# Infini-attention and a GELU FFN on one core: small operations moved off VectorE, first tiles projected in five parts, 64-row rests of twelve weight tiles in one bracket

## The chip, the cores and the metric

The kernel runs on one core of one Trainium2 chip. A core has TensorE (PE: matmuls and transposes, which write into eight PSUM banks of 128 x 2 KB), VectorE (DVE), ScalarE (ACT: activations from tables that must be loaded), GpSimd (POOL) and SyncE (SP), which issues most of the DMAs here. The metric is the time of one execution in microseconds (us). Every time below is the chip's, from timed runs or from one profiled execution.

## The reference

Input x is 2048 x 576 in bf16. LN is a layer norm without weights. There are 32 heads of 18, and the rows are cut into four segments of 512.

```python
def _A_ref(x, wq, wk, wv, wo, beta):
    q, k, v = (heads(x @ w) for w in (wq, wk, wv))       # heads() stands for reshape and transpose
    phi = lambda t: jnp.where(t > 0, t + 1.0, jnp.exp(t))
    g = _sigmoid(beta).reshape(1, H, 1, 1)
    for s in range(N):                                   # the four segments, M and z start at 0
        logits = einsum('bhqd,bhkd->bhqk', qs, ks) * scale + mask
        a_dot = einsum('bhqk,bhkd->bhqd', _softmax(logits), vs)
        a_mem = einsum('bhld,bhde->bhle', phi(qs), M) / (einsum('bhld,bhd->bhl', phi(qs), z)[..., None] + 1e-06)
        outs.append(g * a_mem + (1.0 - g) * a_dot)
        M = M + einsum('bhld,bhle->bhde', phi(ks), vs)
        z = z + einsum('bhld->bhd', phi(ks))
    return concat(outs) @ wo

h  = x + _A_ref(LN(x), wq, wk, wv, wo, beta)
h2 = h + (gelu(LN(h) @ w1 + b1) @ w2 + b2)               # w1 576 x 4608, w2 4608 x 576
```

## The kernel before

**Units.** The rows are cut into 8 chunks of 256, two tiles of 128 rows each; a segment is two chunks. A contraction over 576 is four blocks of 128 rows and a rest of 64. `mm5` (L720 to 723) is such a group: four matmuls of 128 rows (L722) and one for the rest (L723). F1 (the product with w1) is computed transposed: 36 column tiles of w1 times 256 rows of x make a chunk's hT; what the code calls a half is two of those tiles in one PSUM bank, ten matmuls of 128x256, and its eviction adds b1 (L1284 by ScalarE, L1286 by VectorE). F2 then contracts 36 blocks of hT with w2, 288 columns at a time (L1376).

**Streams.** The kernel is a planner. Python generators emit operations: P (LN, transposes, projections of a tile), K and M (phi(k) and the memory's sums), A (scores L957, exp L974, mask L978, weighted values L997), the recall from memory (L1026 to L1034) and what ends a block (L1043 to L1053), B (output projection, residual, second LN), F1 and F2. Each operation has a planned duration and a due time (the tables SLACK, PHASES and LATE). `step` takes the earliest due operation of a ready engine; `either` (L471) gives an eviction to VectorE or ScalarE, whichever is planned to be free first. At the end all operations are issued in the order of their planned start under a manual schedule, so every engine's order is fixed when the program is built, and the waits between engines follow from which tile each operation reads and writes.

**PSUM.** Scores of a visit fill st4, one tile of four banks. `ox` and `bank0` to `bank2` are tiles of one bank each; projections, transposes, F1, F2 and the output projection take turns on bank0 to bank2, and on ox once attention is finished.

**Row tiles.** Score matmuls use 32 rows of the array at a time, a 64-row rest can use 64 (`Half.tail`, L1214; two tiles of weights sit at rows 0 to 63 and 64 to 127). Ten times a pair of halves puts its rests (`pair.tails`) next to a score visit and its full matmuls (`Half.main`, L1220) behind. All other halves compute the rest as a fifth full matmul over rows that are zero in the weights.

**Head.** While nothing is ready in the first microseconds, TensorE multiplies zeros (L1424). x of the first tiles, wq, wk and wv arrive by SP's queue; LN is two bn_stats, bn_aggr (L733), two small operations on VectorE (L734, L735), a power on GpSimd (L740) and the normalisation on VectorE (L743) or ScalarE (L748). In either case one more small copy repeats 64 columns (L745). The normalised tile is transposed by TensorE for the first tiles (pe_x and its like in SLACK say how many) and by a DMA for the others. A tile's projection is four groups of 432 columns; their evictions are at L844 to L854, the transposes of Q and K at L874 and the copies out at L877. Zeros for the paddings are written by GpSimd and VectorE (`memset`, L625). The memory's mask (`maskcol`, `gmzm`) is applied at L926 and after.

**Weights.** w2 stays in SBUF. w1 comes again for each chunk, 512 columns at a time (L1192: 512 KB, L1195: twice 32 KB), two buffers deep, five in the first chunk.

Of the kernel before, what the change touches and what calls it, by code (L numbers as in the profile page):

```python
# [8 lines left out]
ACT = mybir.ActivationFunctionType  # L9
# [7 lines left out]
def kernel(  # L17
# [41 lines left out]
    def sbuf(name, shape, dt=BF16):  # L59
# [13 lines left out]
    SLACK = dict(head=2.35, lnp=15.71, lnb=4.06, pow=-3.98, apply=7.94, ek_k=78.96, relu_k=-8.71, min_k=3.71,  # L73
                 add_k=10.93, mz=14.56, exp=16.96, ek=21.6, relu=47.98, min=14.06, add=31.72, hb=57.84,
                 gelu=30.88, finish=-1.23, mem=0.08, sum=20.21, out=3.91, hd=34.06, xp=-29.81, xb=-19.31,
                 t_x=23.19, t_q=37.57, t_k=38.16, t_o=-3.03, t_h=19.9, w1=3.76, w2=33.77, hc=-2.46, evict=-17.31,
                 qk=7.8, ot=-7.54, mask=0.42, lead=1.57, balance=22.63, b1=11.77, zeros=6.77, hold=0.62,
                 delay=0.92, pe_x=2, pe_q=3, pe_k=2, pe_o=2, pe_h=1, d_x1=1.69, d_wk=-5.24, marg=0.8, cj=4,
                 flex=1.0, qkv=0.0, flexn=1.0, d_wv=1.68, d_xb=0.5, d_wo=3, d_b2=1.97, bulk=11.07, w2v=5)
    PHASES = [(30.0, dict(exp=38.12, hold=2.18, sum=8.51, lnp=15.18, min_k=9.68, lead=1.93, t_h=47.5, t_o=-3.5,  # L80
                          flexn=1.85, mem=25.71)),
              (60.0, dict(gelu=28.89, apply=7.66, min_k=-36.61, lnp=16.16, w2=14.91, qk=8.17, t_q=37.57, delay=0,
                          hc=9.3)),
              (110.0, dict(t_x=30.47, min=14.15, mz=13.94, hold=5.27, w1=24.51, t_q=28.42, ek=20.74, apply=0.43,
                          pow=-9.03, xp=-16.35, hc=0.85, w2=31.47, out=4.0, bulk=8.26)),
              (200.0, dict(mem=-1.42, w1=12.55, lead=3.33, t_o=-5.89, mask=8.5, finish=-0.41, xb=-20.35, hd=32.92,
                          lnb=4.83, exp=20.2, apply=21.55)),
              (300.0, dict(add_k=6.54, delay=0.17, add=4.0, hd=24.4, mem=3.13, mz=15.86, ek_k=80.69, min_k=14.3,
                          exp=16.63, join=-18.57, qk=4.56, lead=1.87, xp=-30.24, min=9.66, qkv=5.33, t_x=21.9,
                          out=37.08, apply=10.19, hold=0.28))]  # L90
# [81 lines left out]
    def note(o, rd, wr):  # L172
# [5 lines left out]
        for k in rd:  # L178
# [4 lines left out]
        'wqkv0': [0.2],  # L183
        'mhalf': [4.1],
        'wqkv_pad': [4.4],
# [14 lines left out]
        ('x_p', 0): [0, 15.2, 41.5, 77.3, 169.5, 193.4, 233.4],  # L200
        ('qk', 0, 'pad'): [17.5],
        'wqkv1': [1.4],
        ('v1', 0): [22.7],
        ('v1', 1): [26.9],
        'ident': [4.9],
        ('v1', 2): [45.5],
        ('v1', 3): [57.3],
        'wqkv1t': [1],
        ('v1', 4): [60.2],
        ('v1', 5): [67.5],  # L210
        'maskcol': [58.4, 70.6, 62.4, 71.3, 63.8],
        ('qk', 2, 'pad'): [24.9],
        ('x_p', 1): [2, 26.1, 91.6, 103.7, 202.6, 212.6, 294.4],
        ('v1', 6): [123.5],
        'beta': [29.3],
        'wqkv2': [3.5],
        'wqkv2t': [3.7],
        ('o', 0, 'pad'): [27.9],
        ('x_b', 0): [7.6, 30.5, 71.9, 119, 172.9, 230.9, 273.1, 317.9, 377.7],
        ('phik', 0, 'pad'): [32.7],  # L220
        ('wo', 4): [38.2, 44],
        ('phik', 1, 'pad'): [33.8],
        ('w1', 0, 'z', 0): [41.5],
        ('x_b', 1): [10.9, 45, 87.4, 133.1, 201.2, 242.8, 296.4, 330.6, 418],
        ('w1', 0, 'z', 1): [39.6],
        'stp0': [2.8, 3.3, 3.8, 4.3, 11, 11.5, 11.9, 12.5, 21.5, 23.3, 21.5, 22.3, 51.2, 47.3, 36.4, 25.7,
            78.9, 94.5, 95.4, 97.9, 174.1, 174.5, 175, 175.5, 195.3, 194.5, 193.8, 196.7, 244.8, 239.6,
            247.2, 236.5],
        ('w1', 1, 'z', 0): [44.9],
        'b1': [18.1],  # L230
        ('w1m', 2, 'z', 1): [46.3],
        ('wo', 0): [23.5],
        ('w1m', 2, 'z', 0): [59],
        ('w1', 1, 'z', 1): [53.3],
        ('qk', 3, 'pad'): [57.8],
        ('o', 1, 'pad'): [48.3],
        ('xn1', 0): [5, 13.2, 25.8, 49.4, 89.7, 176.2, 197.5, 238.4],
        ('w1m', 3, 'z', 1): [58.4],
        ('w1m', 3, 'z', 0): [58.7],
        ('w1m', 4, 'z', 1): [66],  # L240
        ('xT', 'p', 0): [5.2, 16.9, 22.9, 46.4, 90.3, 177.4, 198.5, 245.7],
        'MZb': [71.1, 69, 72.3, 71.4, 71.7, 76.8, 64.6, 74.2, 62.6, 191.3, 192.4, 192.2, 195.4, 196.6, 197.4,
# [1240 lines left out]
```

## Time and profile before

| | us |
|---|---|
| three timed runs: lowest, median, highest | 476.8, 477.23, 478.39 |
| the profiled execution | 476.5 |
| its span in the trace | 474.8 |
| exp of the scores (L974), 80 on ScalarE | 150.2 busy |
| F2 (L1376), 1044 and more on TensorE | 144.0 busy |
| evictions of F1 (L1286), 130 on VectorE | 89.3 busy, 0.688 each |
| gelu (L1349), 23 on ScalarE | 66.0 busy |

The page's second section cuts the span into 40 slices of 11.9 us and gives busy tenths; these are VectorE's, ScalarE's and GpSimd's:

```profile
DVE  4889996587877476888877556887457646334310
ACT  2578879964678668896789595687457864212210
POOL 9468463295745344786773518665133312000000
```

A digit of 9 is 90% or more. The largest lines of VectorE are the evictions of F1, of ScalarE the exponentials:

```profile
L974 ACT ACTIVATE pt<-st 128x2048 bf16<-128x2048 f32 x80 | 150.2, 1877 | 65.4 <-PE st L957 63.6
L1286 DVE TENSOR_TENSOR hT<-bank,b1T 128x512 bf16<-128x512 f32 x130 | 89.3, 688 | 72.5 <-PE bank L723 65.1
L1043 DVE STREAM_TRANSPOSE ox<-ox 128x512 f32<-128x512 f32 x32 | 23.2, 725 | 11.7 <-PE ox L997 11.1
```

Such a line reads: place in the code, engine, operation, output and input, count; then busy us in all and mean ns of one; then the engine's idle time before them and what ended most of it.

### The profile page before, as it was taken

How to read it: one execution, taken by the hardware profiler on the slowest of the kernel's cores; microseconds unless marked ns; L12 is line 12 of the kernel's file. 1: busy time of each engine (PE TensorE's matmuls, PEld its weight loads, DVE VectorE, ACT ScalarE, POOL GpSimd, SP SyncE). 2: the span in 40 equal slices, each digit the busy share in tenths (PEclk: the TensorE clock that was granted, in tenths of full speed). 3: DMA queues.
4: the chain of work that ended last, by engine and by line, in shares of the span. 5: the costliest groups of instructions: out<-in, count | busy, mean ns of one | idle time of the engine just before them, and what ended most of it. 6: DMA issues, size and time to landing. Idle time of an engine off the chain costs nothing.

```text
span 474.8 us, 14410 instructions
## 1 busy us (share of the span) xinstructions
PE 462.5 (97%) x6056; PEld 350.9 (74%) x6056; DVE 311.4 (66%) x744; ACT 302.9 (64%) x245; POOL 217.2 (46%) x333
## 2 busy tenths in 40 slices
PE   8999999799999999999999999999999999999997
PEld 6655687468777777767768777777877788888875
DVE  4889996587877476888877556887457646334310
ACT  2578879964678668896789595687457864212210
POOL 9468463295745344786773518665133312000000
PEclk9999999999999999999999999999999999999999
DMA  8999799927588577469458559486744655655411
GB/s 240 200 231 206 262 163 295 253 52 165 162 214 218 150 178 185 97 142 199 83 155 204 156 143 193 89 196 187 181 147 135 185 166 158 185 168 164 137 39 50
DMA packets 118881, 79.94 MB, mean 168 GB/s; under 512 B 53344, under 2 KB 116768, under 8 KB 118816
## 3 DMA queue, kind: packets, MB, share of 16 engines
q1 hardware_dynamic: 118784, 79.01, 66.8%
q8 instruction: 47, 0.77, 0.7%
q14 instruction: 18, 0.15, 0.1%
q0 software_dynamic: 32, 0.01, 0.1%
HBM read 60.09 MB, written 7.08 MB: 141 GB/s over the span
## 4 chain that ended last, share of the span: by engine, by line
PE 84%; DVE 6%; ACT 4%; issue 2%; DMA 2%; SPq 1%; ACTq 0%; DVEq 0%
PE bank L722 29%; PE bank L1376 26%; PE bank L723 7%; PE st L957 5%; PE ox L997 4%; PE bank L1220 4%; PE ox L1376 3%; PE st L1424 2%; DMA xT<-xn 2%; ACT pt L974 1%; PE ox L722 1%; PE bank L1026 1%; ACT hT L1349 1%; DVE ox L1043 1%; PE bank L1214 1%
## 5 line engine op out<-in xcount | busy, mean ns | idle before, releaser
L974 ACT ACTIVATE pt<-st 128x2048 bf16<-128x2048 f32 x80 | 150.2, 1877 | 65.4 <-PE st L957 63.6
L1376 PE MATMUL bank<-w_sb,hT 128*128 128x288 bf16 x1044 | 144.0, 286 | 2.1 <-ACT hT L1349 2.1
L1286 DVE TENSOR_TENSOR hT<-bank,b1T 128x512 bf16<-128x512 f32 x130 | 89.3, 688 | 72.5 <-PE bank L723 65.1
L1376 PEld LDWEIGHTS <-hT 128*128 128x128 bf16 x1152 | 110.5, 98 | 31.8 <-ACT hT L1349 2.4
L978 POOL TENSOR_SCALAR_AFFINE_SELECT pt<-pt 128x512 bf16<-128x512 bf16 x128 | 80.4, 643 | 107.1 <-ACT pt L974 105.4
L722 PE MATMUL bank<-xn2T,w1g 128*128 128x256 bf16 (+1 forms) x888 | 122.2, 269 | 1.9 <-DMA w1g<-in_B_w_dram 0.9
L722 PEld LDWEIGHTS <-w1g 128*128 128x128 bf16 x944 | 88.4, 98 | 16.3 <-issue 1.5
L1349 ACT ACTIVATE hT<-hT 128x4608 bf16<-128x4608 bf16 (+5 forms) x23 | 66.0, 2874 | 46.7 <-DVE hT L1286 46.5
L723 PE MATMUL bank<-xn2T,w1g 128*128 128x256 bf16 (+1 forms) x222 | 59.7, 269 | 0.0
L722 PE MATMUL bank<-wqkv,xT 128*128 128x432 bf16 x256 | 57.4, 346 | 1.1 <-DMA xT<-xn 0.8
L722 PEld LDWEIGHTS <-xT 128*128 128x128 bf16 x384 | 34.9, 97 | 23.7 <-DMA xT<-xn 0.9
L1016 POOL TENSOR_TENSOR pq<-ek,pq 128x512 bf16<-128x512 bf16 x24 | 27.9, 1163 | 11.8 <-DVE ek L1014 9.1
L957 PE MATMUL st<-QT,KT 32*128 32x128 bf16 x1280 | 32.2, 217 | 1.2 <-ACT pt L974 1.1
L1043 DVE STREAM_TRANSPOSE ox<-ox 128x512 f32<-128x512 f32 x32 | 23.2, 725 | 11.7 <-PE ox L997 11.1
L1380 DVE TENSOR_TENSOR ot<-bank,hc 128x288 bf16<-128x288 f32 x29 | 13.1, 453 | 25.1 <-PE bank L1376 25.1
L957 PEld LDWEIGHTS <-KT 32*128 32x128 bf16 x1280 | 18.8, 92 | 14.3 <-issue 9.2
L997 PE MATMUL ox<-pt,v_aug 128*19 128x128 bf16 x1280 | 26.5, 220 | 0.0
L997 PEld LDWEIGHTS <-v_aug 128*19 128x19 bf16 x1280 | 17.9, 91 | 10.9 <-issue 10.0
L723 PEld LDWEIGHTS <-w1g 128*128 128x128 bf16 x236 | 23.1, 98 | 2.7 <-DMA w1g<-in_B_w_dram 0.2
L844 ACT CAST qk_pad<-bank 128x432 bf16<-128x432 f32 x28 | 14.5, 522 | 14.3 <-PE bank L723 11.8
L1053 POOL TENSOR_TENSOR o_nat<-t,t 128x288 bf16<-128x288 f32 x24 | 19.6, 816 | 8.3 <-DVE t L1052 7.5
L723 PE MATMUL bank<-wqkv,xT 65*128 65x432 bf16 x64 | 22.2, 348 | 0.0
(124 smaller groups left out, 578.1 us busy)
## 6 DMA issues: line engine op xcount, KB each, us to landing
w1g<-in_B_w_dram SPq DMA_DIRECT2D x67, 512.0 KB, 4.3
w_sb<-in_B_w_dram SPq DMA_DIRECT2D x6, 864.0 KB, 6.9
hd<-h_t SPq DMA_DIRECT2D x16, 288.0 KB, 3.5
hc<-hd SPq DMA_DIRECT2D x32, 144.0 KB, 3.4
w1g<-in_B_w_dram SPq DMA_DIRECT2D x134, 32.0 KB, 3.5
x_b<-in_A_x_dram SPq DMA_DIRECT2D x18, 144.0 KB, 4.4
hT<-in_B_w_dram SPq DMA_DIRECT2D x5, 512.0 KB, 4.8
out_dram<-ot SPq DMA_DIRECT2D x16, 144.0 KB, 1.8
```

What stands on the lines that cost most here:

```text
L722: nc.tensor.matmul(out=out_ap, lhsT=lhsT_of(slice(0, P), k), rhs=rhs_of(slice(0, P), k), start=(k == 0), stop=False)
L723: nc.tensor.matmul(out=out_ap, lhsT=lhsT_of(slice(0, rest), 4), rhs=rhs_of(slice(0, rest), 4), start=False, stop=True)
L957: nc.tensor.matmul(out=st4[:, i, n * P:(n + 1) * P], lhsT=KTs[(2 * (c - c % 2) + kt) % NK][rows, g, :], rhs=QTs[(2 * c + qt) % NQ][rows, g ...
L974: op("ACT", 1.88, lambda: nc.scalar.activation(out=pt[:], in_=st4[:], func=ACT.Exp, scale=scale), sk, [("pt", slot, n) for n in range(4)], ...
L978: op("POOL", 0.65, lambda n=n: nc.gpsimd.affine_select(out=pt[:, :, n * P:(n + 1) * P], in_=pt[:, :, n * P:(n + 1) * P], pattern=[[0, 4], ...
L997: nc.tensor.matmul(out=ox[32 * i:32 * i + E, (g % 4) * P:(g % 4) * P + P], lhsT=v_augs[(2 * s0 + kt) % NV][:, G * i + g, :], rhs=pts[slot] ...
L1016: op("POOL", 1.16, lambda: nc.gpsimd.tensor_tensor(out=pq[:], in0=e_g, in1=pq[:], op=ALU.add), ["ek"], ["pq"], slack=due("add"))
L1043: op("DVE", 0.73, lambda: nc.vector.transpose(out=ox[:], in_=ox[:]), [], ["ox"], slack=slack)
L1053: op("POOL", 0.8, lambda: nc.gpsimd.tensor_tensor(out=o_dst, in0=t1[:].rearrange("p (g b) e -> p g b e", g=4), in1=t2[:].rearrange("p (g b ...
L1286: either((0.684, lambda: nc.vector.tensor_tensor(out=dst, in0=acc, in1=bias, op=ALU.add)), (nj * (0.166 + w * 0.00082), by_act), [b, "b1T" ...
L1349: op("ACT", (f1e - f0) * Q * 0.00083 + 0.18, lambda hT=hT, f0=f0, f1e=f1e: nc.scalar.activation(out=hT[:, f0:f1e, :], in_=hT[:, f0:f1e, :] ...
L1376: nc.tensor.matmul(out=acc, lhsT=hT[:, q, tl * P:(tl + 1) * P], rhs=w2_sb[:, q, hs], start=(q == 0), stop=(q == NF - 1))
```

## The change

- **Layer norm**: the additions of epsilon (32) and the factors for ScalarE (15) move from VectorE to GpSimd, the repeated 64 columns to GpSimd or ScalarE. More normalisations go to ScalarE.
- **Memory**: the mask is replaced by sums that are prepared with zeros and 1e-6, so that the masked products and the additions before the reciprocal go (24 and 12 operations of VectorE).
- **Zeros**: `zero` lets ScalarE copy zeros out of `pq` where GpSimd is planned to be later.
- **Head**: the first two tiles are projected in five parts, of 432, 432, 288, 144 and 432 columns, in that order of weights (Q, K, the rest of both, the rest of V, V). One more xT, three more QT and two more xn2T tiles are transposed by TensorE. x of the second tile is the second transfer; beta comes by SP's queue. The evictions of Q and K and the copies of xT may go to either engine. The first gelu takes 18 tiles or more as soon as they are there.
- **Rests**: once attention is finished, the four banks of st4 join the slots, and F1 takes `wide` (6) halves at a time in the last two chunks: the 64-row rests of twelve weight tiles stand in one bracket, then the halves' full matmuls. In these chunks w1 is five buffers deep, three of them over wqkv.
- Due times and planned durations are set anew (SLACK, PHASES, LATE; not shown), and `step` may leave an engine idle for an operation that is due earlier and planned to be ready soon (`look`).

In the changed kernel's numbering: `zero` L722, LN L775 to L804, projections L768 and L769, evictions of Q and K L894 to L911, scores L1014, exp L1029, values L1052, rests L1274, full matmuls of such halves L1280, F1's eviction L1375 (VectorE), gelu L1391, F2 L1488, zero matmuls L1552.

```diff
--- before.py
+++ after.py
...
 
 
         (d, go_d), (a, go_a) = dve, act
-        if behind("ACT") + a + due("flex") < behind("DVE") + d:
-            return op("ACT", a, go_a, rd, wr, slack)
-        return op("DVE", d, go_d, rd, wr, slack)
+        if behind("ACT") + a + due("flex") + more < behind("DVE") + d:
+            return op("ACT", a, go_a, rd, wr, slack, tag=tag)
+        return op("DVE", d, go_d, rd, wr, slack, tag=tag)
...
     banks["ox"] = ox
+    for j in range(4):
+        banks["st", j] = st4[:, j, :]
...
+    W0 = (NCH - 2) * NG
+    done_w = wqkv[:].rearrange("p k n -> p (k n)")
+    w1_late = [done_w[:, j * KT * 512:(j + 1) * KT * 512].rearrange("p (k f) -> p k f", f=512) for j in range(3)]
+
     def w1_of(n):
 
 
         if n < NG and n % 5 > 1:
             return w1_more[n % 5 - 2], ("w1m", n % 5)
+        if n >= W0:
+            j = (n - W0) % 5
+            if j > 1:
+                return w1_late[j - 2], ("w1l", j)
+            j = (W0 - NG + j) % 2
+            return w1_bufs[j], ("w1", j)
...
+        def zero(pool, act, ap, rows, shape, key, slack):
+            if behind("ACT") + due("flexz") < behind("POOL"):
+                src = flat[rows, 0:shape[0]] if len(shape) == 1 else flat[rows, 0:shape[0] * shape[1]].rearrange("p (a b) -> p a b", b=shape[1])
+                op("ACT", act, lambda: nc.scalar.copy(out=ap, in_=src), ["pq"], [key], slack)
+            else:
+                memset("POOL", pool, ap, 0.0, key, slack)
...
             for h in range(2):
-                memset("POOL", 0.3, w1_of(n)[0][64 - 64 * h:P - 64 * h, 4, 256 * h:256 * h + 256], 0.0, (*w1_of(n)[1], "z", h), slack=due("zeros"))
-        memset("POOL", 0.95, MZ_blk[:], 0.0, "MZb", slack=7)
+                rows = slice(64 - 64 * h, P - 64 * h)
+                zero(0.33, 0.43, w1_of(n)[0][rows, 4, 256 * h:256 * h + 256], rows, (256,), (*w1_of(n)[1], "z", h), due("zeros"))
...
-        def first():
-            nc.vector.bn_aggr(out=mv[:], in_=stats[:])
-            nc.vector.tensor_scalar(out=rstd[:], in0=mv[:, 1:2], scalar1=EPS, scalar2=None, op0=ALU.add)
-            nc.vector.tensor_scalar(out=nmr[:], in0=mv[:, 0:1], scalar1=-1.0, scalar2=None, op0=ALU.mult)
+        def power():
+            nc.gpsimd.tensor_scalar(out=rstd[:], in0=mv[:, 1:2], scalar1=EPS, scalar2=None, op0=ALU.add)
+            nc.gpsimd.tensor_tensor(out=rstd[:], in0=rstd[:], in1=mhalf[:], op=ALU.pow)
...
+        late = slack + due("apply")
+        waiting = {"DVE": behind("DVE"), "ACT": behind("ACT") + due("flexn")}
+        by = min(waiting, key=waiting.get)
+        if by == "ACT":
+            op("POOL", 0.26, lambda: nc.gpsimd.tensor_scalar(out=nmr[:], in0=mv[:, 0:1], scalar1=rstd[:], scalar2=-1.0, op0=ALU.mult, op1=ALU.mult),
+               [], ["st" + who], slack=slack + due("pow"))
+            op("ACT", 0.86 if f32 else 0.66, lambda: nc.scalar.activation(out=dst[:, 0:D], in_=src, func=ACT.Identity, bias=nmr[:], scale=rstd[:]),
+               ["st" + who, skey], [dkey], slack=late)
+        else:
+            op("DVE", 0.65, apply, ["st" + who, skey], [dkey], slack=late, port=True)
+        if f32:
+            if behind("ACT") + due("flexd") < behind("POOL"):
+                op("ACT", 0.22, lambda: nc.scalar.copy(out=dst[:, D:XW], in_=dst[:, 512:D]), [], [dkey], slack=late, tag="again")
+            else:
+                op("POOL", 0.25, lambda: nc.gpsimd.tensor_copy(out=dst[:, D:XW], in_=dst[:, 512:D]), [], [dkey], slack=late, tag="again")
...
-                wk = wk + WALL[6:]
+            for ch in (0, 1, 4, 5, 3) if t < SLACK["spl"] else range(4):
+                wk = {0: WALL[0:2], 1: WALL[2:4], 2: WALL[0:6], 3: WALL[4:6], 4: WALL[0:4], 5: WALL[4:6]}[ch] + WALL[6:]
+                nw = {4: 288, 5: 144}.get(ch, CH)
                 yield need(None, bank_slots, [kx] + wk)
...
+                if c == NCH - 1:
+                    for n in range(W0 + 2, W0 + 5):
+                        for h in range(2):
+                            memset("POOL", 0.3, w1_of(n)[0][64 - 64 * h:P - 64 * h, 4, 256 * h:256 * h + 256], 0.0,
+                                   (*w1_of(n)[1], "z", h), slack=due("zeros"), more=WALL)
+                        load_w1(n, WALL)
...
-                if c == 0:
-                    op("DVE", 0.42, lambda acc=acc, mz=mz: nc.vector.tensor_copy(out=acc, in_=mz), [b], ["MZacc"])
-                else:
-                    op("DVE", 0.45, lambda acc=acc, mz=mz: nc.vector.tensor_tensor(out=acc, in0=acc, in1=mz, op=ALU.add), [b], ["MZacc"])
+                op("DVE", 0.46, lambda acc=acc, mz=mz: nc.vector.tensor_tensor(out=acc, in0=acc, in1=mz, op=ALU.add), [b], ["MZacc"])
...
+                    op("DVE", 0.49, lambda rows=rows, i=i, mzb=mzb: nc.vector.tensor_tensor(
+                        out=mzb[rows, :, 32 * i:32 * i + E], in0=MZacc[rows, :, E * i:E * i + E], in1=gmz[rows, :, :],
+                        op=ALU.mult), ["MZacc", "gmz"], ["MZb"], slack=due("mz"))
...
-        op("DVE", 0.175, lambda: nc.vector.tensor_scalar(out=r2[:], in0=omv[:, :, Dh], scalar1=1e-6, scalar2=None, op0=ALU.add),
-           [b], ["r2"], slack=due("mem"))
-        op("DVE", 0.25, lambda: nc.vector.reciprocal(out=r2[:], in_=r2[:]), [], ["r2"], slack=due("mem"))
+        op("DVE", 0.25, lambda: nc.vector.reciprocal(out=r2[:], in_=omv[:, :, Dh]), [b], ["r2"], slack=due("mem"))
...
         bank_slots.free.append("ox")
+        for i in range(4):
+            bank_slots.free.append(("st", i))
...
-            self.keys = keys
-            self.halves = [Half(f_slots.take(), c, jp + i) for i in range(2)]
+        def __init__(self, c, jp, keys, n=2, slots=None, attached=False):
+            self.keys, self.lent, self.attached = keys, slots is not None, attached
+            self.halves = [Half(slots[i] if slots else f_slots.take(), c, jp + i) for i in range(n)]
+
+        def tails(self):
+            for i in range(0, len(self.halves), 2):
+                for a in range(2):
+                    for half in self.halves[i:i + 2]:
+                        half.tail(a)
...
+            def gelu(c, f0, f1e, hT=hT):
+                alone = NCH - 1 in done_A
+                if f1e - f0 < (6 if alone else 18 if c else SLACK["gp0"]) and f1e < NF:
+                    return f0
+                op("ACT", (f1e - f0) * Q * 0.00083 + 0.18, lambda: nc.scalar.activation(
+                    out=hT[:, f0:f1e, :], in_=hT[:, f0:f1e, :], func=ACT.Gelu_apprx_tanh),
+                   [], [("hT", c % 2, q) for q in range(f0 // 2, f1e // 2)], slack=0 if alone else due("gelu"), table="gelu")
+                return f1e
...
+                            f0 = gelu(c, f0, 4 * n + 4)
...
+                count = 0
+                if ("st", 0) in bank_slots.free:
+                    count = min(SLACK["wide"], NF // 2 - jp, 6 if c * NG >= W0 else 4 if jp % 2 == 0 else 2)
+                if count > 1 and count % 2 == 0:
+                    keys = xk + [k for j in range(0, count, 2) for k in wkeys(c * NG + (jp + j) // 2)] + wkeys(c * NG + (jp + count - 1) // 2)
+                    groups = range(c * NG + jp // 2, c * NG + (jp + count - 1) // 2 + 1)
+                    yield need(lambda: go_on() and loaded.issuperset(groups), f_slots, keys, n=count)
+                    pair = Pair(c, jp, keys, count)
...
+                    count = len(pair.halves)
+                    if not pair.attached:
+                        op("PE", 0.12 * count, pair.tails, pair.keys, [h.b for h in pair.halves], mode="half")
...
-                jp += 2 if pair else 1
+                        if m < W0:
+                            load_w1(m + 2 if m >= NG else {0: 5, 1: 6, 2: 7, 3: 8, 5: 9, 6: 10}.get(m))
+                        else:
+                            load_w1(m + 5)
```

More of the change, by code (lines that the diff above doesn't have):

```diff
@@ L72 @@
     PVS = 2
[L73 to L79, printed above, removed]
@@ L213 @@
[L213 to L224, printed above, removed]
@@ L737, in layernorm @@
         half(0)
         half(1)
[L739 to L741 removed]
+        op("DVE", 0.22, lambda: nc.vector.bn_aggr(out=mv[:], in_=stats[:]), [], ["st" + who], slack=slack)
+        op("POOL", 0.82, power, ["mhalf"], ["st" + who], slack=slack + due("pow"))
         def apply():
             nc.vector.tensor_scalar(out=dst[:, 0:D], in0=src, scalar1=mv[:, 0:1], scalar2=rstd[:], op0=ALU.subtract, op1=ALU.mult)
[L744 to L745 removed]
@@ L747, in apply_by_act @@
-        def apply_by_act():
-            nc.scalar.activation(out=dst[:, 0:D], in_=src, func=ACT.Identity, bias=nmr[:], scale=rstd[:])
-            if f32:
-                nc.scalar.copy(out=dst[:, D:XW], in_=dst[:, 512:D])
-        if behind("ACT") + due("flexn") < behind("DVE"):
-            op("POOL", 0.2, lambda: nc.gpsimd.tensor_tensor(out=nmr[:], in0=nmr[:], in1=rstd[:], op=ALU.mult), [], ["st" + who], slack=slack + due("pow"))
-            op("ACT", 0.86 if f32 else 0.64, apply_by_act, ["st" + who, skey], [dkey], slack=slack + due("apply"))
-            return
@@ L962, in go @@
             if pair is not None:
-                for a in range(2):
-                    for half in pair.halves:
-                        half.tail(a)
+                pair.tails()
             for n in range(4):
@@ L1135, in stream_A @@
         bank_slots.free.append("ox")
+        for i in range(4):
+            bank_slots.free.append(("st", i))
     def stream_B(tl):
@@ L1252, in holds @@
         if g is F1:
-            return getattr(waits[g], "pair", None) is not None and visit_when() <= now + due("hold")
+            return getattr(waits[g], "pair", None) is not None and visit_when() <= now + due("hold") and not quad()
+        if g is A and getattr(waits[g], "group", False):
+            return tiles != "row" and now < ready("PE", (), [("st", i) for i in range(4)]) <= now + due("hpv")
         if g is A:
@@ L1265, in open_pair, with quad, open_quad @@
         return p
+    def quad():
+        offer = getattr(waits.get(F1), "pair", None)
+        if offer is None or ("st", 0) in bank_slots.free or len(done_B) - work["F1"] / 18 <= due("qlead"):
+            return False
+        c, jp = offer
+        if c == 0 or jp % 2 or jp + 3 >= NF // 2 or not loaded.issuperset((c * NG + jp // 2, c * NG + jp // 2 + 1)):
+            return False
+        keys = pair_keys(c, jp) + pair_keys(c, jp + 2)
+        lent = [("st", i) for i in range(4)]
+        if ready("PE", keys, lent) > now:
+            return False
+        return c, jp, keys, lent
+    def open_quad():
+        q = quad()
+        if q:
+            c, jp, keys, lent = q
+            f1["pair"] = Pair(c, jp, keys, 4, lent)
+            waits[F1] = next(F1)
+        return bool(q)
     def stream_F1():
@@ L1400, in step @@
                 if can:
-                    begin(min(can, key=lambda o: (o.due, o.made)))
+                    o = min(can, key=lambda o: (o.due, o.made))
+                    if e != "SP":
+                        soon = [p for p in queue[e] if p.due < o.due - 1 and now < p.ready() <= now + due("look")]
+                        if soon:
+                            t = min(p.ready() for p in soon) + 0.03
+                            can = [p for p in can if now + p.dur <= t]
+                            if not can:
+                                continue
+                            o = min(can, key=lambda o: (o.due, o.made))
+                    begin(o)
                     return True
@@ L1409, in step @@
         order = ffn + first if len(done_B) - work["F1"] / 18 > due("lead") else first + ffn
+        if quad():
+            order = [F1] + [g for g in order if g is not F1]
+        if tiles in ("col", "row") and A in waits:
+            order = [A] + [g for g in order if g is not A]
         for held in (False, True):
@@ L1413, in step @@
                     changes += 1
+                    if g is F1 and free_at["PE"] <= now and open_quad():
+                        changes += 1
+                        return True
                     try:
```

414 lines of the change are left out of this document (235 added, 179 removed), and 301 rows, old and new, of the table LATE.

## The prediction

> **What bounds the kernel now.** I first read the page's busy times and slices, for the bounding engine:
>
> ```profile
> PE 462.5 (97%) x6056; PEld 350.9 (74%) x6056; DVE 311.4 (66%) x744; ACT 302.9 (64%) x245; POOL 217.2 (46%) x333
> ...
> PEclk9999999999999999999999999999999999999999
> ```
>
> TensorE works 97% of the span at the full granted clock; VectorE, from which the change takes work, stands at 66%. So the second view is the table of windows, for where TensorE has idle time at all. Its columns are window, length, busy PE, PE loads, DVE, ACT, POOL, granted clock, DMA share, GB/s:
>
> ```profile
> 20.00:70.00 50.00, 47.63 (x855) 32.06 (x855) 44.89 (x113) 40.76 (x44) 34.02 (x54) 1.00 0.97 208
> 100.00:400.00 300.00, 299.19 (x4085) 227.79 (x4083) 212.60 (x497) 214.23 (x162) 156.19 (x229) 1.00 0.65 160
> 400.00:470.00 70.00, 70.00 (x600) 58.48 (x598) 21.97 (x37) 13.62 (x10) 1.29 (x1) 1.00 0.46 137
> ```
>
> From 100 us on TensorE is never free. In 20 to 70 us VectorE (44.89 of 50) and the DMAs (0.97) run beside a TensorE that misses 2.4 us. The view of waits, first 100 us, says on what:
>
> ```profile
> PE bank L1376 <- ACT hT L1349: 2.1, 1, 2.1
> PE bank L722 <- DMA w1g<-in_B_w_dram: 0.9, 1, 0.9
> PE bank L722 <- DVE MZacc L926: 0.8, 1, 0.8
> PE bank L722 <- DMA xT<-xn: 0.8, 1, 0.8
> ```
>
> Adding start-to-start distances of all 6056 matmuls in the timeline (0.109 us for a 128x256, 0.1225 for a 128x288, 0.182 for a 128x432, 0.0555 for a 128x128, about 0.092 extra at each change between full tiles and row tiles) splits the span: 1.3 start, 421.4 work, 236 changes at 0.092 = 21.7, 11.2 of zero matmuls that fill waits, 15.5 lost (10.2 of it before 100 us), 3.8 after the last matmul. So VectorE's relief can pay only out of some 21 us, in the head; after 100 us only TensorE's own stream counts.
>
> **The sum, part by part.** It is made against the profiled execution, 476.5 us (span 474.8 and 1.7 around it); the median shown is 0.7 higher, added at the end.
>
> *Rests of 12 weight tiles in one bracket.* The order of the changed program has six such brackets in the last two chunks: the 64-row rests of six halves, two at once, then the six halves' full tiles. A half before is ten 128x256 starts. Per bracket 12 starts go (12x0.109=1.31); six pairs (0.118 a pair, from rows of L1214) and two mode changes (0.18) come: -0.41. Six make **-2.4**. The trace has ten pairs that stand beside score visits, which the new order keeps; those change nothing. The Trainium skill, "TensorEngine Tiling (Array Packing)", section Key Properties, says that a change of tiling mode drains TensorE. If a drain cost a matmul's whole 0.27 us instead of my 0.092, the twelve changes would cost about 2 us more and eat this gain; the distances in the trace speak for the small price.
>
> *What the six brackets wait for.* The halves need six banks, and the change takes four of them from the scores' tile st4 (free once attention is over). The order of the changed program, with its waits, shows this in each bracket (runs joined, row numbers left out):
>
> ```
> L1280 Matmult ox, x8
> L1280 Matmult bank2, x8
> L1280 Matmult st4, x12
> L1280 Matmult st4 [waits DVE]
> ...
> ```
>
> and twice more, 8 matmuls apart. st4 is one tile of four banks: a bank's eviction by VectorE and the next half's matmuls into another bank count as the same tile. The eviction of half k is issued behind the first four matmuls of half k+1 and waits for them; the second four wait for that eviction. So every half in st4 but the bracket's first stalls TensorE, which runs in order: the rest of the bracket, all F2 tiles and, at last, the end stand behind it. Six brackets with three waits: 18. Before, halves rotate through separate tiles, and nothing waits:
>
> ```profile
> 448.44 0.60 PE L722 MATMUL bank<-xn2T,w1g 128*128 128x256 bf16 x4
> 448.88 0.27 PE L723 MATMUL bank<-xn2T,w1g 128*128 128x256 bf16 x1
> 449.19 0.69 DVE L1286 TENSOR_TENSOR hT<-bank,b1T 128x512 bf16<-128x512 f32 x1 [1.61 <-PE bank L723]
> ```
>
> That is the row to price the cycle: the last matmul's 0.27, then 0.04 until VectorE starts (448.88+0.27=449.15, start 449.19), 0.69 for the eviction, and 0.06 back to TensorE, from this pair (20.99+0.69=21.68 to 21.74):
>
> ```profile
> 20.99 0.69 DVE L877 COPY QT<-bank 128x1024 bf16<-128x1024 bf16 x1 [0.91 <-PE bank L874]
> 21.74 0.49 PE L1424 MATMUL bank<-pq 128*128 128x256 bf16 x3 [0.22 <-DVE QT L877]
> ```
>
> 0.27+0.04+0.69+0.06 = 1.06, less the 0.109 at which the next start would come anyway: 0.95 a wait. 18x0.95=17.1. Two more such places stand around the only other use of st4 after attention (the last output projections, L1218, and a bracket of four): one at 0.95 and two at 0.72 (an addition of 0.455 in place of 0.69), 2.4. Together **+19.6**. Bounds: if an eviction could start right behind its own half, the wait would be 1.06 less five starts, 0.52: 18x0.52 and 1.2 make 10.6. If another VectorE operation (0.453, an output addition) came between each time, it would be 18x0.453 more; the order puts one only between brackets, and I take a third of it as the upper bound, 22.3. I take 0.95, since the semaphore order makes it. The waits for ScalarE on some evictions (gelu has left the buffer) are far ahead, as F2 stands between.
>
> *The head (up to 100 us).* Off VectorE: 32 rstd and 15 nmr operations (0.15), 16 xn copies (0.43) to GpSimd, 24 additions (0.17) and 12 masks (0.38), 12 LN applies and the head's zeros (0.2 to 0.5 each) to ScalarE: some 25 us, of which I put 10 before 100 us, by where these lines stand in the timeline. GpSimd (34.0 of 50 in the stretch) and ScalarE (40.8) have room; the zeros stand before their first real work, behind the DMAs. The gelu wait (2.1): the order now puts 11 groups of five matmuls between chunk 0's last eviction and F2's first tile, so it goes: -2.1. The waits for DMA (w1 0.9, hT 0.6): the zeros that these loads stand behind no longer queue on VectorE and GpSimd: -1.0. xT by DMA 0.8: the three first tiles transpose on TensorE: -0.8. MZacc 0.8: -0.4, half, since VectorE's queue thins by about a quarter. Against: 39 more transposes at 0.0555 = 2.2, of which I let 1.0 be covered by waits the zeros now fill: +1.2; wv goes behind 648 KB moved ahead of it, landing some 2.3 us later by the rate of the other loads, mostly under the projections in five parts that need only wq and wk first: +0.3; x1 second on SP's queue delays wq by about 0.6 (144 KB at 240 GB/s), under zeros, since the first projection's input is bound by LN: 0; w2's six loads move ahead of chunk 1's w1 on SP and have 20 us of slack: 0. Sum -2.8, rounded **-3.0**; the zero matmuls stay (76 before, 80 now in the order), so the first microseconds win nothing. Bounds: -6 (all waits above and half the zeros' excess) to +2 (only the transposes come).
>
> *100 to 400 us.* TensorE busy 99.7%; moved DVE work hides under it: 0, and costs nothing as long as ScalarE (71%) isn't last: 0 +-2.
>
> 476.5 - 2.4 + 19.6 - 3.0 = 490.7; +0.7: **491.4**.
>
> **Rivals.** (1) *Waits at half price*: evictions aren't tied to the next half in practice; 18x0.52+1.2=10.6, so 482.4. For: the lower bound; against: the waits in the order. (2) *Clock falls*: three idles of 0.95 within some 5 us, six times, and the clock drops to the half pace of the first 26 zeros (5.61/26=0.216 against 0.109). Were a stretch of 3.4 us at that pace for each bracket, half of it would be lost: 1.7x6 = 10 us, 501. Against: 2.09 us of idle for gelu (to 93.53 in the timeline) was followed by matmuls at 0.1225. The Trainium skill, "TensorE: Matmul & The Clock Gate", section A second HAM failure mode: psum-queue depth-cycling, says that micro-idles between matmul groups can make the clock oscillate; no row here does. (3) *Not slower*: the head wins what the brackets lose. It has 21 us of zeros and waits; from 17.2 on (19.6-2.4) the kernel is not slower; if all 21 went, 473.4. For: VectorE and DMA near saturation there. Against: 80 zeros are still in the order. (4) *The relief does nothing*: head at 0, its transposes paid by its waits, 494.4; inside the forecast's range.
>
> **Chances.** Forecast (with 4) 0.78, own range 485 to 498; half price 0.11; clock 0.07; not slower 0.04. The range 482 to 499 takes in both bounds of the wait with the head's middle, and leaves out the clock and the rest. This kernel's measurement can tell about 0.3% from no change (475.8 to 478.7): faster 0.03, same 0.03, slower 0.94.
>
> **What would show it.** The view of waits, after 370 us: PE L1280 waiting for DVE L1375 some 18 to 20 times at 0.9 to 1.0; busy PE in the last slices at 80 to 90% instead of full; evictions of st starting only behind the next half's first four matmuls. In the head no gelu wait, a smaller sum of waits. Wrong if TensorE's last 100 us stay gapless (then about 472), or if the head still loses 10 us (then 494), or if distances of 0.2 us show a falling clock.

## The result, and the profile after

The changed kernel takes 488.77 us (median of four runs, 488.25 to 489.25); the kernel before took 477.73 beside it (476.8 to 478.39). The ratio is 1.0232, 95% interval 1.021 to 1.0255: slower by 11.0 us, against 14.2 forecast. The profiled execution took 488.81 (span 487.1), 12.3 above that of before.

The page's busy times and slices are the first to read, as before:

```profile
PE 464.7 (95%) x6109; PEld 349.2 (72%) x6109; DVE 295.3 (61%) x629; ACT 310.9 (64%) x261; POOL 226.9 (47%) x391
...
PE   8999999999999999999999999999998889888897
...
PEclk9999999999999999999999999999999999999999
```

VectorE went from 311.4 to 295.3 us busy, 16.1 less; the prediction counted some 25 us of operations that leave it. TensorE's busy time is about what it was (464.7, 462.5 before), its share fell from 97% to 95%, and the slices show where: from slice 31 on (some 365 us) 8 stands where 9 stood. The clock is full throughout. The windows (columns as in the prediction) say the same in numbers:

```profile
20.00:70.00 50.00, 48.70 (x875) 32.85 (x876) 40.20 (x93) 39.62 (x38) 35.47 (x58) 1.00 0.94 217
...
400.00:470.00 70.00, 59.69 (x513) 47.02 (x513) 21.19 (x33) 13.35 (x9) 0.00 (x0) 1.00 0.33 100
```

In the head TensorE is busy for 48.70 of 50 us (47.63 before), with VectorE at 40.20 (44.89). Between 400 and 470 us, where it was busy for all 70.00, it now works 59.69. TensorE's waits from 365 us to the end name the reason (line waited in, what it waited for, us in all, times, longest):

```profile
PE st L1280 <- DVE hT L1375: 14.2, 18, 0.9
PE st L1280 <- DVE h_t L1218: 1.1, 2, 0.5
PE st L768 <- DVE hT L1375: 0.9, 1, 0.9
```

Before 100 us the waits for gelu, w1, hT, MZacc and xT that the prediction quoted are gone from the list; the largest left is 1.3, for the very first zeros, which the kernel before had too.

One bracket in the timeline, TensorE's rows (start, duration, line and operation, matmuls, idle time ahead and what ended it):

```profile
408.46 0.60 PE L1274 MATMUL st<-xn2T,wqkv 64*128 64x256 bf16 x8
408.99 1.05 PE L1280 MATMUL ox<-xn2T,w1g 128*128 128x256 bf16 x8
409.87 1.04 PE L1280 MATMUL bank<-xn2T,w1g 128*128 128x256 bf16 x8
410.75 1.47 PE L1280 MATMUL st<-xn2T,wqkv 128*128 128x256 bf16 x12
413.00 1.03 PE L1280 MATMUL st<-xn2T,wqkv 128*128 128x256 bf16 x8 [0.78 <-DVE hT L1375]
414.82 1.03 PE L1280 MATMUL st<-xn2T,wqkv 128*128 128x256 bf16 x8 [0.78 <-DVE hT L1375]
416.63 0.60 PE L1280 MATMUL st<-xn2T,wqkv 128*128 128x256 bf16 x4 [0.78 <-DVE hT L1375]
```

The halves in `ox` and `bank2` run on. In st, twelve matmuls start (a half and the first four of the next), then a wait, then eight and a wait, twice more. VectorE's rows of the same stretch:

```profile
412.26 0.69 DVE L1375 TENSOR_TENSOR hT<-st,b1T 128x512 bf16<-128x512 f32 x1 [0.62 <-PE st L1280]
414.07 0.69 DVE L1375 TENSOR_TENSOR hT<-st,b1T 128x512 bf16<-128x512 f32 x1 [1.12 <-PE st L1280]
```

The first half in st had its last start at about 411.5 (eight matmuls from 410.75), yet its eviction starts at 412.26, when the twelfth matmul has ended (410.75+1.47=412.22): it waited for four matmuls into another bank. TensorE starts again at 413.00, 0.05 behind the eviction's end at 412.95. The idle time of 0.78 that the row shows is counted from the modelled end of the last matmul; by starts a wait costs 0.946 us (0.78, and the 0.27 of that matmul less the 0.109 at which the next would have started).

### The profile page after: what moved, and what is told of

It is laid out like the page before. It is cut to its first block, busy times and chain, and to the rows that moved or that the text cites. A ratio compares the mean times of both kernels' runs of the same rounds, so it can differ in the third digit from the quotient of the medians.

```text
span 487.1 us, 14428 instructions
## 1 busy us (share of the span) xinstructions
PE 464.7 (95%) x6109; PEld 349.2 (72%) x6109; DVE 295.3 (61%) x629; ACT 310.9 (64%) x261; POOL 226.9 (47%) x391
## 4 chain that ended last, share of the span: by engine, by line
PE 94%; DVE 4%; ACT 1%; issue 1%; DVEq 0%; ACTq 0%
PE bank L768 29%; PE bank L1488 28%; PE bank L769 7%; PE st L1014 5%; PE st L1280 5%; PE bank L1280 5%; PE ox L1052 5%; DVE hT L1375 3%; PE st L1552 2%; PE ox L1280 1%; PE bank L1081 1%; PE st L1488 1%; PE ox L1488 1%; PE bank L979 1%; ACT pt L1029 1%; PE bank L1274 1%
## 5 line engine op out<-in xcount | busy, mean ns | idle before, releaser
L1029 ACT ACTIVATE pt<-st 128x2048 bf16<-128x2048 f32 x80 | 150.2, 1878 | 58.8 <-PE st L1014 55.8
L1488 PE MATMUL bank<-w_sb,hT 128*128 128x288 bf16 x1080 | 146.9, 286 | 0.0
L1488 PEld LDWEIGHTS <-hT 128*128 128x128 bf16 x1152 | 111.1, 98 | 28.2
L1391 ACT ACTIVATE hT<-hT 128x1536 bf16<-128x1536 bf16 (+5 forms) x25 | 66.5, 2661 | 79.0 <-DVE hT L1375 78.9
L1375 DVE TENSOR_TENSOR hT<-bank,b1T 128x512 bf16<-128x512 f32 x107 | 73.4, 686 | 42.6 <-PE bank L769 28.8
L768 PE MATMUL bank<-xn2T,w1g 128*128 128x256 bf16 (+1 forms) x640 | 87.3, 268 | 0.0
L768 PEld LDWEIGHTS <-w1g 128*128 128x128 bf16 x640 | 58.3, 98 | 10.6
L768 PE MATMUL bank<-wqkv,xT 128*128 128x432 bf16 (+2 forms) x252 | 55.5, 342 | 0.1
L768 PEld LDWEIGHTS <-xT 128*128 128x128 bf16 x392 | 35.6, 97 | 23.9 <-issue 1.8
L769 PE MATMUL bank<-xn2T,w1g 128*128 128x256 bf16 (+1 forms) x160 | 42.8, 267 | 0.0
L1280 PEld LDWEIGHTS <-w1g 128*128 128x128 bf16 x304 | 28.4, 98 | 13.1 <-issue 9.0
L1014 PE MATMUL st<-QT,KT 32*128 32x128 bf16 x1280 | 32.2, 217 | 0.3
L1375 DVE TENSOR_TENSOR hT<-st,b1T 128x512 bf16<-128x512 f32 x26 | 18.0, 692 | 22.9 <-PE st L1280 21.8
L1014 PEld LDWEIGHTS <-KT 32*128 32x128 bf16 x1280 | 18.8, 92 | 13.7 <-issue 8.9
L1052 PE MATMUL ox<-pt,v_aug 128*19 128x128 bf16 x1280 | 26.7, 220 | 0.4 <-issue 0.4
L1052 PEld LDWEIGHTS <-v_aug 128*19 128x19 bf16 x1280 | 17.9, 91 | 11.2 <-issue 10.3
L1280 PEld LDWEIGHTS <-wqkv 128*128 128x128 bf16 x160 | 15.3, 97 | 13.0 <-issue 11.3
```

The source lines that it names most:

```text
L768: nc.tensor.matmul(out=out_ap, lhsT=lhsT_of(slice(0, P), k), rhs=rhs_of(slice(0, P), k), start=(k == 0), stop=False)
L769: nc.tensor.matmul(out=out_ap, lhsT=lhsT_of(slice(0, rest), 4), rhs=rhs_of(slice(0, rest), 4), start=False, stop=True)
L1014: nc.tensor.matmul(out=st4[:, i, n * P:(n + 1) * P], lhsT=KTs[(2 * (c - c % 2) + kt) % NK][rows, g, :], rhs=QTs[(2 * c + qt) % NQ][rows, g ...
L1029: op("ACT", 1.88, lambda: nc.scalar.activation(out=pt[:], in_=st4[:], func=ACT.Exp, scale=scale), sk, [("pt", slot, n) for n in range(4)], ...
L1052: nc.tensor.matmul(out=ox[32 * i:32 * i + E, (g % 4) * P:(g % 4) * P + P], lhsT=v_augs[(2 * s0 + kt) % NV][:, G * i + g, :], rhs=pts[slot] ...
L1280: nc.tensor.matmul(out=self.acc[:, a, :], lhsT=self.wt[:, k, f:f + P], rhs=xn2T[self.c % 4][:, k, :], start=False, stop=(k == 3), skip_gro ...
```

## The experiments

Each ratio is to the kernel before, run on the same chip. "Lost" is the prediction's accounting of start distances: what is neither work, nor a mode change, nor zeros.

**Own tiles.** The order stays; at the first use of a lent bank the scores' tile is given up, and four tiles of one bank take its place. Operations look their bank up when they are issued (not shown).

```diff
-    st4 = ps.tile([P, 4, 512], F32, name="st4")
+    score_pool = tc.alloc_tile_pool(name="score_pool", bufs=1, space=PSUM)
+    st4 = score_pool.tile([P, 4, 512], F32, name="st4")
...
+    class Banks(dict):
+        def __missing__(self, key):
+            score_pool.release()
+            late = tc.alloc_tile_pool(name="late", bufs=1, space=PSUM)
...
+            for j in range(4):
+                self["st", j] = late.tile([P, 512], F32, name=f"late{j}")
+            return self[key]
...
-    for j in range(4):
-        banks["st", j] = st4[:, j, :]
```

> The changed kernel, but once attention is finished the scores' tile of four banks is given up and four tiles of one bank each take its place; every engine's order stays as it was. My theory (the stalls come from the shared tile): the 18 waits of TensorE on F1's evictions in the brackets (0.946 us each by start distances in the changed kernel's trace, 17.0) and the three around the last output projections (1.01, 0.71, 0.71) go, nothing takes their place: 488.8-19.5 = 469.3, faster than before by 1.7%. Rival one (VectorE can't evict six halves as fast as TensorE fills them, or the bracket itself costs the time): the stalls stay at some other line, 485 to 489. Rival two (the late banks come with a wait of their own, for the whole tile to be given up): one wait of 1 to 2 us, 470 to 472.

Measured: 468.58 us (468.21 to 470.5), ratio 0.9806 (0.9785 to 0.9826). A second time, beside other kernels:

> Own tiles once more, as the control beside the next run, since the chip of the last four gave the kernel before a wider spread (476.0 to 484.1). Both theories of the brackets expect the ratio of the first time, 0.981 of before.

Measured: 471.63 (468.17 to 471.8, in two groups, 468 to 470 and 471.6 to 471.8), ratio 0.9842 (0.9814 to 0.9869). The expected 0.981 lies just below this interval, since the median fell into the upper group. The list of TensorE's waits behind 100 us is empty in both traces. The same bracket in the second one:

```profile
400.68 1.04 PE L1291 MATMUL bank<-xn2T,w1g 128*128 128x256 bf16 x8
401.56 3.66 PE L1291 MATMUL late<-xn2T,wqkv 128*128 128x256 bf16 x32
405.05 6.04 PE L1499 MATMUL bank<-w_sb,hT 128*128 128x288 bf16 x48
```

```profile
402.63 0.69 DVE L1386 TENSOR_TENSOR hT<-late,b1T 128x512 bf16<-128x512 f32 x1 [0.18 <-PE late L1291]
403.50 0.69 DVE L1386 TENSOR_TENSOR hT<-late,b1T 128x512 bf16<-128x512 f32 x1 [0.18 <-PE late L1291]
404.38 0.69 DVE L1386 TENSOR_TENSOR hT<-late,b1T 128x512 bf16<-128x512 f32 x1 [0.18 <-PE late L1291]
```

Thirty-two matmuls into the four late banks run through without a gap, and the evictions follow at 0.87 us, a half's length, with 0.18 of idle: VectorE keeps up. So neither the bracket nor VectorE's speed was the trouble but the one tile. The late banks bring no wait of their own: in this trace the last exp of scores starts at 359.0 and takes 1.88 us, and the first matmul into a late bank starts at 365.8.

**No lending, no brackets.**

```diff
-        for i in range(4):
-            bank_slots.free.append(("st", i))
```

> The changed kernel without lending the scores' four banks: no brackets either, the last two chunks' halves are ten full matmuls each, as before. My theory: the waits go with the lending and the brackets' gain with them: 488.8-19.5+2.4 = 471.7, which is what the head and the rest of the change are worth by themselves (477.7 before). Rival (the head won nothing, the rest of the difference is brackets): 477 to 478.

Measured: 473.51 (472.29 to 474.0), ratio 0.9908 (0.9885 to 0.993): 1.8 us above my 471.7 and well below the rival's 477, so the rest of the change gains by itself. By start distances in the traces, work and mode changes take 445.07 us here and 442.52 in own tiles: the brackets are worth 2.55 (76 full matmuls against as many rests, two at once, and 14 mode changes). The timed ratios lie 0.7 to 1.0% (3 to 5 us) apart; they bear out the sign, and with their intervals they allow the 2.55 without showing it.

**Mixed.** The lent banks stay one tile, but in each bracket a half in st alternates with one in a bank of its own.

```diff
-                    for i, half in enumerate(pair.halves):
+                    lent = [i for i, h in enumerate(pair.halves) if h.b[0] == "st"]
+                    rest = [i for i in range(count) if i not in lent]
+                    turns = [i for p in zip(lent, rest) for i in p] + lent[len(rest):] if len(lent) == 4 else range(count)
+                    for i in turns:
+                        half = pair.halves[i]
```

> The changed kernel with its lent banks as they are, and another order of the full matmuls in each bracket: a half in the scores' tile, one in a bank of its own, and so on, the last two in the scores' tile. If the price of a wait is the cycle last matmul 0.27, 0.04, eviction 0.69, 0.06, less what TensorE can start meanwhile, a half of 0.87 between leaves 1.06-0.87-0.11 = 0.08 of it: per bracket 0.08, 0.08 and 0.95 instead of three of 0.946, so 18 waits cost 6.7 instead of 17.0: 478.5. If the wait's price doesn't depend on what stands between (a fixed cost of the semaphore or of changing the bank): 488.8 again.

Measured: 478.8 (478.06 to 481.61), ratio 1.0027 (1.0005 to 1.0049). The waits behind 375 us:

```profile
PE st L1280 <- DVE hT L1375: 4.8, 6, 0.9
```

One wait a bracket is left, the one between the two st halves at its end, at the old price (4.8/6 = 0.8 of idle). The other twelve are down to 0.08 by starts, as in the bracket that begins at 405 us:

```profile
406.69 1.04 PE L1280 MATMUL ox<-xn2T,w1g 128*128 128x256 bf16 x8
407.64 1.03 PE L1280 MATMUL st<-xn2T,wqkv 128*128 128x256 bf16 x8
```

From the half in `ox` to the next one in st it is 0.95, where eight matmuls at 0.109 make 0.87. The price is the cycle of eviction and semaphores less what TensorE may do meanwhile, as the sum had it.

**The head: old numbers of transposes.** From here on the edits are made to own tiles.

```diff
-                 delay=1.78, pe_x=3, pe_q=6, pe_k=2, pe_o=1, pe_h=3, d_x1=1.39,
+                 delay=1.78, pe_x=2, pe_q=3, pe_k=2, pe_o=1, pe_h=1, d_x1=1.39,
```

> Own tiles again, and the head's transposes as before the change: two tiles' xT, three QT and one xn2T by TensorE, the others by DMA. It takes the 39 transposes (2.2 us of TensorE) off again. Against own tiles: if the head's waits went because of these transposes, they come back, at least the 0.8 for xT by DMA and more behind it: 1 to 3 us slower. If the transposes bought nothing (the waits went with VectorE's and ScalarE's shorter queues): 1 to 2.2 us faster. My step said they cost 1.2 and bring 0.8: within 0.5 of own tiles.

Measured: 476.37 (474.52 to 479.12), ratio 0.998 (0.9951 to 1.0009). All three expectations missed. The plan was made anew by this edit, and its order lost time in many places (21.1 us lost, 8 to 9 in own tiles), also behind 100 us, where no transposes had changed. The run doesn't tell the transposes from the order, so the next ones keep the order.

**The head, part by part, in one order.** Three edits change what an operation issues and leave its place in the plan; a fourth has all three. One piece of each:

```diff
-            nc.gpsimd.tensor_scalar(out=rstd[:], in0=mv[:, 1:2], scalar1=EPS, scalar2=None, op0=ALU.add)
...
+            nc.vector.tensor_scalar(out=rstd[:], in0=mv[:, 1:2], scalar1=EPS, scalar2=None, op0=ALU.add)
+            nc.vector.tensor_scalar(out=nmr[:], in0=mv[:, 0:1], scalar1=-1.0, scalar2=None, op0=ALU.mult)
...
-                op("ACT", act, lambda: nc.scalar.copy(out=ap, in_=src), ["pq"], [key], slack)
+                op("ACT", act, lambda: nc.gpsimd.memset(ap, 0.0), ["pq"], [key], slack)
...
+                turn = lambda xTt=xTt: nc.sync.dma_start_transpose(out=xTt[:], in_=xn1[tl][:])
```

> Own tiles (468.6) with 120 small operations put back on VectorE where the change took them away (epsilon, the factor for ScalarE, the repeated columns, the addition before the reciprocal, the mask as two products), with every engine's order otherwise as it is. By their durations before, 32x0.15+16x0.15+16x0.43+24x0.17+12x0.23: about 21 us of VectorE. My theory (VectorE is off the path; only the head can feel it, by the 0.4 that I gave to MZacc's wait): 468.6 to 470. Rival (the head's 5 to 7 us came from VectorE's relief): 473 to 476.

> Own tiles with the 11 groups of zeros that ScalarE copies written by GpSimd instead, at the same places of the order. My step gave them 1.0 (TensorE's waits for w1 and hT, 1.5 before, whose loads stand behind zeros): 469.6. Rival (they are behind other work anyway): 468.6. Second rival (GpSimd delays the first masks and with them the scores): 471 and more.

> Own tiles with the 39 transposes that the change added on TensorE (one xT, three QT, two xn2T) done by DMA on SP's queue at the place where their copies stood; the order of all other work is unchanged. It tells what the transposes buy from what the plan's new order does, which the run with the old counts mixed (476.4). My step: they cost 1.2 and bring 0.8, so within 0.5 of 468.6. Rival (a transfer of some 6 us, as the 6.12 us of xT by DMA in the first trace's chain, puts TensorE in wait each time): up to six waits of 1 to 4 us, 472 to 480.

> Own tiles with all three parts of the head put back at once in the same order (VectorE's 120 small operations, the zeros by GpSimd, the 39 transposes by DMA); the five-part projections, the order and the brackets stay. By the spans of the single runs against own tiles without its 1.2 us of a stall that no engine explains (467.6): 2.6 + 4.3 + 3.5 = 10.4, a span of 478, if the parts add up. If they hide behind one another (each wait of TensorE needs only one late input): 472 to 475. Before with brackets alone would stand at 477.7-2.5 = 475.2: if this kernel is above that, the new order needs the relief; if it is clearly below, the order and the five parts are worth something by themselves.

| put back | time, us | ratio to before | span | lost | zeros |
|---|---|---|---|---|---|
| nothing (own tiles, both traces) | 468.58, 471.63 | 0.9806, 0.9842 | 468.8, 466.5 | 9.3, 7.8 | 12.1, 11.4 |
| VectorE's 116 operations | 473.25 | 0.9897 (0.9863 to 0.993) | 470.2 | 10.2 | 12.7 |
| zeros by GpSimd | 473.7 | 0.9912 (0.9879 to 0.9944) | 471.9 | 10.6 | 13.9 |
| 39 transposes by DMA | 475.2 | 0.9922 (0.9887 to 0.9956) | 471.1 | 13.7 | 12.1 |
| all three | 474.89 | 0.994 (0.992 to 0.996) | 471.7 | 11.2 | 14.8 |

Times are medians, spans those of the one profiled execution. By spans the parts are worth 1.4 to 3.7, 3.1 to 5.4 and 2.3 to 4.6 us (the two traces of own tiles are the ends), each more than my steps gave it, and together 2.9 to 5.2: they don't add up, the second alternative of the last expectation. In the head one late input hides another. The three times lie in the ranges of rivals, not of my steps (for the zeros by layer norms, as shown below, where the rival named the first masks). Own tiles did not run on the chip of the three single parts, so the ratios are the safer measure: 0.6 to 0.9%, 0.7 to 1.1%, 0.8 to 1.2%, and 1.0 to 1.3% for all three. The interval of VectorE's part (from 0.9863) overlaps that of the second own tiles (to 0.9869), so this one is not clear of noise.

VectorE's part is 116 operations (745 on VectorE against 629; the expectation says 120): 32 epsilons, 32 factors, 16 copies, 24 additions before the reciprocal and 12 masked products. They make 14.8 us of VectorE (309.7 against 294.9), not 21, and GpSimd is relieved of 12.7 (214.3 against 227.0); the run shows the net of both.

The last expectation had a second question, whether the order and the five parts are worth something by themselves. With all three parts back the ratio is 0.994 (0.992 to 0.996), and before with brackets alone would be 475.2 of 477.7, 0.995: nothing beyond noise. The head's gain needs these three parts; the new order and the five parts alone don't show one.

How the zeros cost: with them on GpSimd, its rows of the first microseconds show layer norms standing between memsets.

```profile
8.38 0.67 POOL L730 MEMSET w1g<- 64x256 bf16 x2
9.03 0.21 POOL L787 TENSOR_SCALAR rstd_p<-mv_p 128x1 f32<-128x1 f32 x1
...
12.25 0.66 POOL L730 MEMSET hT<- 64x256 bf16 x2
12.89 0.21 POOL L787 TENSOR_SCALAR rstd_p<-mv_p 128x1 f32<-128x1 f32 x1
```

In own tiles (second trace) these two layer norms start at 5.74 and 8.14. The third tile's is 4.75 us later, so its normalised rows are, and TensorE waits for them to transpose. The first tile is late too: its layer norm starts at 6.32 (4.27 in own tiles), its normalisation on VectorE ends at 7.23+0.68 = 7.91, and its transposes follow (5.66 in own tiles), though the row names another releaser:

```profile
7.23 0.68 DVE L796 TENSOR_SCALAR xn<-x_p,mv_p,rstd_p 128x576 bf16<-128x576 bf16 x1 [2.28 <-POOL rstd_p L788]
7.96 0.45 PE L817 MATMUL bank<-ident,xn 128*128 128x128 bf16 x5 [1.77 <-POOL MZacc L655]
14.91 0.45 PE L817 MATMUL bank<-ident,xn 128*128 128x128 bf16 x5 [2.02 <-DVE xn L796]
```

And the transposes: six DMAs stand in their place, and the longest of TensorE's waits by far is for the third tile's xT, which took 4.3 us from issue to landing. TensorE's order is fixed, so all its work stands behind this wait:

```profile
17.65 0.54 PE L776 MATMUL bank<-wqkv,xT 128*128 128x432 bf16 x2 [3.47 <-DMA xT<-xn]
```

In own tiles that projection starts at 13.48.

**Four parts instead of five.**

```diff
-                 ... qka=12.45, spl=2, qlead=9, ...
+                 ... qka=12.45, spl=0, qlead=9, ...
```

> Own tiles with the first two tiles projected in four parts as before; the plan is made anew, with 50 halves in pairs instead of 58 (the last bracket's share, 0.4 to 0.8 us, is lost with them). My step gave the five parts nothing but cover for wv's late arrival (0.3): 469 to 470. Rival (the parts are what keeps TensorE fed until wv lands, some 2 us later than before): 471 to 473.

Measured: 480.38 (479.42 to 484.82), ratio 1.0041 (1.0006 to 1.0076), span 479.1, 20.3 us lost. Far outside both expectations, and inconclusive: the plan was made anew, and between 100 and 225 us alone 11.4 us are lost, mostly in waits for VectorE's evictions (two for the residual's addition into `h_t` make 2.0), where the first tiles' projections are long done. As with the old transposes, the due times were laid down for one sequence of operations, and another sequence got a poor order from them.

## Why the prediction was right, and where its sizes were off

- **What bounds it**: right. TensorE's stream decided. Behind 100 us the lost time besides the stalls went from 5.2 to 4.0 us, inside the 0 +-2.
- **The brackets, -2.4**: 2.55 by the accounts of no lending against own tiles. In the second trace of own tiles six pairs of rests and the change back take 0.76 us (399.04 to 399.80), where my prices make 0.80. The drain that the Trainium skill states for a change of tiling mode ("TensorEngine Tiling (Array Packing)", section Key Properties) thus costs here no more than the 0.092 that I read from the rows.
- **The brackets' waits, +19.6**: 19.5. Eighteen at 0.946 make 17.0 (17.1 forecast at 0.95; two of them took 0.07 more), and the three around the last output projections 1.01, 0.71 and 0.71 (2.4 forecast). The lower bound of 0.52 (half price) does not occur; mixed shows what sets the price, and own tiles that it goes with the shared tile. The upper bound's other VectorE operation came between nowhere.
- **The clock**: 18 idles of 0.78 left the granted clock at 1.00, and the matmuls behind them kept 0.109. The rival is out. The Trainium skill tells of a kernel whose clock oscillated by micro-idles between matmul groups ("TensorE: Matmul & The Clock Gate", section A second HAM failure mode: psum-queue depth-cycling); this one's did not.
- **The head, -3.0**: right in its sum, by luck, since its parts were off in both directions. For the first 100 us the accounts give -5.7 of waits (10.2 us lost before; after, 28.0 less 19.5 and less the 4.0 behind 100 us leave 4.5), +2.2 of transposes and +0.5 of zeros, all of which lie before 100 us: -3.0. I had -4.3, +1.2, and +0.3 for wv, for which no wait is in the list. The five waits that I named have 5.2 us of idle in the list and cost 6.0 by start distances, and I let 0.9 of them stand; the scores' wait for exp (0.7 in the list) went as well. The transposes cost their whole 2.2, where I let 1.0 be covered. The reasons were also partly wrong. I gave ScalarE's zeros 1.0 for w1 and hT, and the runs show that it is GpSimd's layer norm that they set free. I gave the transposes a net loss of 0.4, and by spans they win 2 to 5. I gave VectorE's relief 0.4, and by spans it is 1.4 to 3.7. That the gelu wait went by the order is not shown by a run of its own; it was back (2.4) when the plan was made anew with the old transposes.
- **What no term held**: the rest of the difference is 12.3-19.5+2.55 = -4.6, so 1.6 lies outside the head. Of this, 1.2 is the lost time behind 100 us, which I put at 0; some 0.4 of work and of the end after the last matmul I can't place.
- **Not slower**: this rival needed 17.2 us out of the head; 3.0 came, 4.6 with the rest. **No relief** (494.4, the head at 0) is 5.6 us too high; no lending, too, shows a gain without brackets.

So the mechanism was right, and its main term to 0.1 us. Of the 2.6 us by which the forecast was too high, 1.2 lie behind 100 us, 0.7 are the step from the profiled execution to the median, which this time lay together (488.81 and 488.77), and the rest is spread over brackets, waits and work.

## What to carry to other kernels

Before a wide tile's parts are lent out as separate buffers, look at what the waits are attached to: an eviction of one bank and matmuls into the next stalled each other at 0.946 us a time, only because both banks belonged to one tile, and four tiles in the same place made a loss of 2.3% a gain of 1.6 to 1.9%. The order of the program with its waits shows such a pair without a run: a wait between two instructions that touch no common bank. When a part of a head is judged, change what an operation issues and keep the order; two edits that let the plan be made anew (old transposes, four parts) told only how the order suffered.

## What was not expected of the hardware

- Own tiles, the same program on the same chip, took 468.2 to 469.5 or 471.6 to 471.8 us, at a granted clock of 0.996 to 1.000. Its two traces (466.5 and 468.8) come from two chips; they differ by 1.3 us in one gap between weighted values at 43 us, ended by no engine, and by 0.8 in zeros. What sets either is open.
- A GpSimd memset of 128x448 took 0.47 us and two of 64x256 took 0.67. The layer norm's two operations there take 0.8, so the 20 memsets that ScalarE's copies had spared GpSimd (411 operations against 391, 233.7 us against 227.0) are much on one queue.
